# Order of the first token norms, and one token load on ScalarE's queue, in a gated mix of a spectral filter and a token MLP

## The chip, the cores and the metric

The kernel runs on one core of one Trainium2 chip. The metric is the time of one execution on the device in microseconds; the median of several runs is given. The profile is of one further execution, whose span is counted from its first to its last instruction.

## The reference

One tensor of tokens, `x = A_x`, `[1, 2048, 512]` in bfloat16, goes through two branches, a spectral filter over tokens and channels and an MLP over the tokens, and the results are mixed by a gate for each token. Cut to what matters:

```python
x = A_x
g = sigmoid((x * gate_w).sum(-1, keepdims=True))
X = rfft2(x) * (A_w_r + 1j * A_w_i)           # spectral filter
a = irfft2(X, s=(2048, 512))
h = layernorm(x, axis=-1)                   # over the 512 channels, eps 1e-5
u = gelu(einsum("bsd,sf->bdf", h, B_w1) + B_b1) # over the 2048 tokens, f = 1792
b = (einsum("bdf,fs->bds", u, B_w2) + B_b2).transpose(0, 2, 1)
out = g * a + (1 - g) * b
```

The other input `B_x` is not read. The kernel loads the tokens once, through the view `xv`.

## The kernel before

The 2048 tokens are 16 blocks of 128, one token to a partition, 512 channels along the free dimension. Blocks 0 to 7 lie in the buffer `xa` (`xh[0]` in the code), 8 to 15 in `xb`. `load_x(b0, b1)` loads token blocks, `load_w1a(b0, b1)` the rows of `B_w1` for the same blocks and the first 1,024 of its 1,792 columns. All these loads are written out by hand, in the order in which they are to be issued, on SyncE's (SP's) queue. ScalarE's queue carries one small load ahead of them, the first bias `brow`, and near the end one store. Loads share eight completion semaphores in turn, so a load waits, before it is issued, for the landing of the load eight before it.

The order on every engine is the order in which the program calls its instructions (`manual_schedule`). What happens first, and is touched by the change:

- TensorE runs a few matmuls on zeros (`pw`), then `mm1(b, ft)` (line 275) for the blocks 0 to 11 in order: eight matmuls of 128x512 for each block, which need the normalised tokens `hn[:, b]` and the block's weights `w1a`. The last four blocks follow, then the rest of the products and the transforms of the spectral branch, all in one hand-made interleaving (`fill`, `fill_to`, `token`, `dpass`, `inverse`).
- VectorE makes the sums of a block (`bstat`, line 246, `bn_stats` over 512 channels) and aggregates them into mean and variance (`bn_aggr`).
- For the blocks 0 and 1 the root of the variance is taken by ScalarE (line 299, `Sqrt`), and the reciprocal by VectorE (line 304). ScalarE then loads another table (line 306, for `Sin`), and computes angles for the transforms (lines 308 and 309).
- For the later blocks `aggr` (lines 251 to 258) adds epsilon (line 255) and GpSimd takes the power -1/2 (line 258).
- The blocks 0 to 5 are normalised by VectorE (`norm_dve`, line 271; `NDVE` is 6), the blocks 6 to 15 by ScalarE in pairs (`norm`, lines 264 and 267).

The loop over the first two blocks (lines 296 to 305) puts the sums of block 2 between the root of block 1 and its reciprocal: its last lines for block 1 are `bstat(2)`, the reciprocal, and `norm_dve(1)`. After it `aggr(2, 3)` follows, and a loop in which the sums of block b + 1 stand ahead of the norm of block b.

Of the kernel before, what the change touches and what calls it, by code (L numbers as in the profile page):

```python
# [12 lines left out]
F32 = mybir.dt.float32  # L13
I32 = mybir.dt.int32

P = 128
# [6 lines left out]
NDVE = 6  # L23
# [20 lines left out]
def kernel(  # L44
# [13 lines left out]
    nc = tc.nc  # L58
# [5 lines left out]
    small = ctx.enter_context(tc.tile_pool(name="small", bufs=1))  # L64
# [3 lines left out]
    def H(i, shape, name, dt=BF16):  # L68
        return big.tile(shape, dt, tag=f"h{i}", name=name)
# [11 lines left out]
    xv = A_x[0].rearrange("(b a) d -> a b d", a=P)  # L81
    w1v = B_w1.rearrange("(b a) f -> a b f", a=P)
    w2v = B_w2.rearrange("(ft f) s -> f ft s", f=P)
    xh = [H(0, [P, 8, D], "xa"), H(1, [P, 8, D], "xb")]
# [4 lines left out]
    def load_x(b0, b1):  # L89
        nc.sync.dma_start(out=xh[b0 // 8][:, b0 % 8:(b1 - 1) % 8 + 1], in_=xv[:, b0:b1])  # L90

    def load_w1a(b0, b1):
        nc.sync.dma_start(out=w1a[b0 // 4][:, b0 % 4:(b1 - 1) % 4 + 1], in_=w1v[:, b0:b1, 0:FT1 * P])  # L93
# [27 lines left out]
    nc.scalar.dma_start(out=brow[:], in_=B_b1.rearrange("(ft f) -> ft f", f=P))  # L121
    load_w1a(0, 1)
    load_x(1, 2)
    for b in range(1, 3):
        load_x(b + 1, b + 2)
        load_w1a(b, b + 1)
    load_x(4, 6)
    load_w1a(3, 4)
    load_x(6, 8)
# [97 lines left out]
    stats = small.tile([P, NB, nc.vector.BN_STATS_DIM], F32, name="stats")  # L227
    mv = small.tile([P, NB, nc.vector.BN_AGGR_DIM], F32, name="mv")
# [16 lines left out]
    def bstat(b):  # L245
        nc.vector.bn_stats(out=stats[:, b, :], in_=xh[b // 8][:, b % 8, :])  # L246

    def on_dve(b):
        return b <= NDVE or b == NB - 2

    def aggr(b0, b1):
        for b in range(b0, b1):
            nc.vector.bn_aggr(out=mv[:, b, :], in_=stats[:, b, :])
        eng = nc.vector if on_dve(b0) else nc.gpsimd
        eng.tensor_scalar(mv[:, b0:b1, 1], mv[:, b0:b1, 1], 1e-5, 0.0, op0=Alu.add, op1=Alu.add)  # L255
        if not on_dve(b0):
            nc.gpsimd.tensor_scalar(nmr[:, b0:b1], mv[:, b0:b1, 0], -1.0, 0.0, op0=Alu.mult, op1=Alu.add)
        nc.gpsimd.tensor_tensor(rstd[:, b0:b1], mv[:, b0:b1, 1], c_mhalf.to_broadcast([P, b1 - b0]), op=Alu.pow)  # L258
# [11 lines left out]
    def norm_dve(b):  # L270
        nc.vector.tensor_scalar(hn[:, b, :], xh[0][:, b, :], mv[:, b, 0:1], rstd[:, b:b + 1],  # L271
                                op0=Alu.subtract, op1=Alu.mult)
# [14 lines left out]

    sink = small.tile([P, 1], F32, name="sink")
    nc.scalar.activation(sink[:], consts[:, 5:6], ActF.Sqrt, bias=consts[:, 5:6], scale=1.0)
    for v in range(2):  # L290
        nc.vector.tensor_scalar(md[:, v], lrow[:], acol[:, 1:2], 768.0 * v, op0=Alu.mult, op1=Alu.add)


    bcol = small.tile([P, NFT + NB], F32, name="bcol")
    b1f, b2f = bcol[:, 0:NFT], bcol[:, NFT:]
    for b in range(2):
        bstat(b)
        nc.vector.bn_aggr(out=mv[:, b, :], in_=stats[:, b, :])
        nc.scalar.activation(rstd[:, b:b + 1], mv[:, b, 1:2], ActF.Sqrt, bias=consts[:, 5:6], scale=1.0)
        if b == 0:  # L300
            nc.scalar.copy(b1f, pb[:, 0:NFT])
        else:
            bstat(2)
        nc.vector.reciprocal(rstd[:, b:b + 1], rstd[:, b:b + 1])
        norm_dve(b)
    nc.scalar.activation(sink[:], consts[:, 2:3], ActF.Sin, bias=c_mpi, scale=0.0)
# [2 lines left out]
    nc.scalar.activation(mc[:], acol[:, 0:1], ActF.Identity, bias=consts[:, 4:5], scale=1024.0)  # L309


    aggr(2, 3)
    for b in range(2, NDVE):
        bstat(b + 1)
        norm_dve(b)
        if b + 1 < NDVE:
            aggr(b + 1, b + 2)
    for b in range(NDVE, NB, 2):
        if b > NDVE:
            bstat(b)  # L320
        if b == NDVE + 2:
            norm(b - 2, b)
            sines_d()
        bstat(b + 1)
        aggr(b, b + 2)
        if b == NDVE:
            mask(md[:], 1024)
        if b == NB - 2:
            angles_a(1)
        if b > NDVE:  # L330
            norm(b, b + 2)
        if b == NB - 6:
            angles_a(0)
            sines_a(0)
# [4 lines left out]
    for q in range(4):  # L339
# [8 lines left out]
                                in_=TD[:].rearrange("p s t k -> p (s t k)"))  # L348
    nc.sync.dma_start_transpose(out=TB[:].rearrange("p s t k -> p (s t) k"),
                                in_=TA[:].rearrange("p s t k -> p (s t k)"))  # L350
# [445 lines left out]
    b = NB - 1  # L796
# [36 lines left out]
```

## Time and profile before

| | |
|---|---|
| median of 3 runs | 128.57 us (128.41 to 129.02) |
| the profiled execution | 128.94 us |
| its span | 127.2 us, granted clock 1.0 |
| TensorE busy | 122.1 us (96%) |
| VectorE busy | 111.4 us (88%) |
| ScalarE busy | 89.6 us (70%) |
| GpSimd busy | 39.3 us (31%) |
| DMA | 24.05 MB, mean 189 GB/s |

Lines of the profile name an engine, a line of the kernel, the operation, what it writes and reads, and its form; in a timeline the first two numbers are the start and the length in microseconds from the span's start, and a row that ends in "x3" holds three instructions. Square brackets give the idle time ahead of it and what ended that. A matmul's drawn end is modelled and lies beyond the point at which the next one may start: matmuls of 128x512 follow each other every 0.216 us, while each is drawn 0.38 long. PE is TensorE, DVE VectorE, ACT ScalarE, POOL GpSimd, and SPq or ACTq the queue of an engine that issues a DMA. Landings of loads are the times at which the sixteen DMA engines have raised the load's semaphore.

### The profile page before, as it was taken

Reading aid. Unit: us, or ns where it says so; the run is one execution under the profiler, and the core shown is the slowest. Engines: PE = TensorE matmul, PEld = TensorE weight load, DVE = VectorE, ACT = ScalarE, POOL = GpSimd, SP = SyncE. Lnnn points to the kernel's source line nnn. Section 1 sums busy time; section 2 is a strip of 40 time slices with the busy share of each in tenths; the row PEclk is TensorE's granted clock in tenths of the full one; section 3 lists DMA queues with packets and bytes.
Section 4 is the critical chain, followed back from the end, with each engine's and each line's share of the span. In section 5 each row is a group of like instructions: output and inputs, shape, how many; then the busy total and the mean of one; then the engine's idle time right before and its main releaser. Section 6 shows DMA issues by size and latency. Waiting matters only on the chain.

```text
span 127.2 us, 2074 instructions
## 1 busy us (share of the span) xinstructions
PE 122.1 (96%) x750; PEld 65.1 (51%) x750; DVE 111.4 (88%) x190; ACT 89.6 (70%) x137; POOL 39.3 (31%) x67
## 2 busy tenths in 40 slices
PE   6989999999999999999999999999999999999980
PEld 2234444444444576557764765477644444444570
DVE  3699998999999999999999999999999999992150
ACT  4391299999897689998994799229794599422410
POOL 7124288998839397000030000000000000351200
PEclk9999999999999999999999999999999999999999
DMA  3899999998799999999579306710021101179991
GB/s 103 257 312 384 370 372 350 288 302 273 205 226 177 312 289 293 290 288 290 140 208 295 74 0 179 238 42 0 0 83 45 41 18 48 61 93 209 163 219 24
DMA packets 34635, 24.05 MB, mean 189 GB/s; under 512 B 5536, under 2 KB 32032, under 8 KB 34624
## 3 DMA queue, kind: packets, MB, share of 16 engines
q1 hardware_dynamic: 32516, 21.02, 60.0%
q0 software_dynamic: 1936, 2.76, 13.0%
q10 hardware_dynamic: 172, 0.13, 0.3%
q8 instruction: 6, 0.10, 0.3%
q14 instruction: 5, 0.04, 0.1%
HBM read 19.15 MB, written 3.67 MB: 179 GB/s over the span
## 4 chain that ended last, share of the span: by engine, by line
PE 91%; DMA 3%; DVE 1%; SPq 1%; issue 0%
PE yb L469 36%; PE u L275 20%; PE u L459 16%; PE ivt L658 5%; DMA xa<-in_A_x_dram 3%; PE ivd L674 3%; PE dp L526 3%; PE yb L801 2%; PE tok L517 2%; PE tok L518 2%; SPq L90 1%; DVE stats L246 1%; PE ivt L652 0%; PE tok L514 0%; SPq L93 0%; DVE hn L271 0%
## 5 line engine op out<-in xcount | busy, mean ns | idle before, releaser
L469 PE MATMUL yb<-gl,w2t 128*128 128x512 bf16 x210 | 47.5, 379 | 0.0
L469 PEld LDWEIGHTS <-w2t 128*128 128x128 bf16 x210 | 20.2, 98 | 22.0
L275 PE MATMUL u<-hn,w1a 128*128 128x512 bf16 x128 | 28.3, 382 | 0.5 <-DVE hn L271 0.4
L459 PE MATMUL u<-hn,w1b 128*128 128x512 bf16 x96 | 23.3, 379 | 0.0
L449 ACT ACTIVATE tbv<-yb,ombb,omg 128x512 bf16<-128x512 f32 x15 | 11.6, 775 | 15.6 <-PE yb L469 15.6
L275 PEld LDWEIGHTS <-w1a 128*128 128x128 bf16 x128 | 12.6, 98 | 16.3 <-issue 1.5
L779 POOL DMA_DIRECT2D out_dram<-ap x3 | 4.0, 1528 | 49.3 <-DVE ap L774 45.3
L459 PEld LDWEIGHTS <-w1b 128*128 128x128 bf16 x96 | 9.0, 98 | 8.0
L286 ACT ACTIVATE junk<-prod 128x512 bf16<-128x512 bf16 x16 | 10.1, 631 | 0.3
L355 ACT ACTIVATE gl<-u,bcol 128x512 bf16<-128x512 f32 x14 | 9.2, 687 | 1.3 <-PE u L459 0.8
L630 ACT CAST R<-ivt 128x1024 bf16<-128x1024 f32 x8 | 7.8, 1040 | 2.3 <-PE ivt L658 2.3
L258 POOL TENSOR_TENSOR rstd<-mv,consts 128x2 f32<-128x2 f32 (+1 forms) x9 | 6.3, 703 | 8.2 <-DVE mv L255 8.1
L630 ACT CAST H<-ivd 128x1024 bf16<-128x1024 f32 x7 | 6.9, 1050 | 0.8 <-PE ivd L674 0.8
L246 DVE BATCH_NORM_STATS2 stats<-xa 128x6 f32<-128x512 bf16 x8 | 5.5, 686 | 1.1 <-DMA xa<-in_A_x_dram 1.1
L788 DVE TENSOR_TENSOR tbv<-tbv,ap 128x512 bf16<-128x512 bf16 x3 | 1.3, 425 | 5.7 <-ACT tbv L449 5.7
L267 ACT ACTIVATE hn<-xb,nmr,rstd 128x512 bf16<-128x512 bf16 x8 | 5.8, 800 | 0.0
L548 DVE TENSOR_TENSOR tatb<-PMA,wn 128x1024 bf16<-128x1024 bf16 x8 | 5.0, 690 | 0.2 <-issue 0.2
L267 ACT ACTIVATE hn<-xa,nmr,rstd 128x512 bf16<-128x512 bf16 x2 | 1.5, 806 | 5.2 <-DVE nmr L264 5.2
L246 DVE BATCH_NORM_STATS2 stats<-xb 128x6 f32<-128x512 bf16 x8 | 5.2, 675 | 0.0
L674 PEld LDWEIGHTS <-R 128*128 128x128 bf16 x64 | 3.8, 98 | 2.5 <-ACT R L630 2.5
L548 DVE TENSOR_TENSOR tatb<-PMB,wn 128x2048 bf16<-128x2048 bf16 x4 | 4.7, 1227 | 0.2
L674 PE MATMUL ivd<-TI,R 128*128 128x128 bf16 x64 | 4.9, 220 | 0.0
(198 smaller groups left out, 224.5 us busy)
## 6 DMA issues: line engine op xcount, KB each, us to landing
w2t<-in_B_w_dram SPq DMA_DIRECT2D x8, 896.0 KB, 9.8
w1b<-in_B_w_dram SPq DMA_DIRECT2D x3, 1024.0 KB, 16.2
w1a<-in_B_w_dram SPq DMA_DIRECT2D x2, 1024.0 KB
out_dram<-tbv SPq DMA_DIRECT2D x14, 128.0 KB, 3.9
out_dram<-ap POOLq DMA_DIRECT2D x3, 512.0 KB, 6.5
w1a<-in_B_w_dram SPq DMA_DIRECT2D x4, 256.0 KB, 4.6
w1a<-in_B_w_dram SPq DMA_DIRECT2D x2, 512.0 KB, 7.9
xb<-in_A_x_dram SPq DMA_DIRECT2D x2, 512.0 KB, 7.2
```

The costliest lines, as they stand in the source:

```text
L246: nc.vector.bn_stats(out=stats[:, b, :], in_=xh[b // 8][:, b % 8, :])
L267: nc.scalar.activation(hn[:, b, :], xh[b // 8][:, b % 8, :], ActF.Identity, bias=nmr[:, b:b + 1], scale=rstd[:, b:b + 1])
L275: nc.tensor.matmul(u1[ft], lhsT=w1a[b // 4][:, b % 4, ft * P:(ft + 1) * P], rhs=hn[:, b, :], start=(b == 0), stop=(b == NB - 1))
L286: nc.scalar.activation(junk[:], prod[b // 8][:, b % 8], ActF.Copy, accum_out=glog[:, b:b + 1])
L355: nc.scalar.activation(gl[:, ft, :], src, ActF.Gelu_apprx_tanh, bias=b1f[:, ft:ft + 1], scale=1.0)
L449: nc.scalar.activation(tbv[0][:, b], y[:], ActF.Identity, bias=gate["ombb2"][:, b:b + 1], scale=gate["omg"][:, b:b + 1])
L459: nc.tensor.matmul(u[:], lhsT=w1b[c][:, b, k * P:(k + 1) * P], rhs=hn[:, b, :], start=(b == 0), stop=(b == NB - 1))
L469: nc.tensor.matmul(y[:], lhsT=w2t[b // 2][:, ft, (b % 2) * P:(b % 2 + 1) * P], rhs=gl[:, ft, :], start=(ft == 0), stop=(ft == NFT - 1))
L548: mul(tt[:, i, :, r:r + n], PM[:, 2 * s:2 * s + 2, r:r + n], w[:, None].to_broadcast([P, 2, n, 256]))
L630: nc.scalar.copy(out, pr[:].rearrange("p h n -> p (h n)"))
L658: nc.tensor.matmul(o[:, 2 * v:2 * v + 2], lhsT=UV[:, 2 * v + c, r, par::2], rhs=TB[:, s, c:c + 2], start=(c == 0), stop=(c == 1))
L674: nc.tensor.matmul(pr[:, c, o * P:(o + 1) * P], lhsT=plane(par, cos), rhs=TI[:, lst, t], start=True, stop=True)
```

## The change

Tokens of block 2 are issued by ScalarE, after its first activation, and leave SP's queue; the weights of block 1 take their place there, one issue earlier. The loop over the first blocks runs over three: block 1 is normalised before the sums of block 2 start, and block 2 takes its root on ScalarE and its reciprocal on VectorE as the first two do. The sums of block 3 are made in two halves of 256 channels in a buffer of their own, `st3`; the first half stands between block 2's aggregation and its reciprocal, the second behind block 2's norm. One `bn_aggr` takes both halves. From block 3 on GpSimd's power is used as before.

```diff
     load_w1a(0, 1)
     load_x(1, 2)
-    for b in range(1, 3):
-        load_x(b + 1, b + 2)
-        load_w1a(b, b + 1)
+    load_w1a(1, 2)
+    load_x(3, 4)
+    load_w1a(2, 3)
     load_x(4, 6)
...
         for b in range(b0, b1):
-            nc.vector.bn_aggr(out=mv[:, b, :], in_=stats[:, b, :])
+            nc.vector.bn_aggr(out=mv[:, b, :], in_=stats[:, b, :] if b != 3 else st3[:])
...
     nc.scalar.activation(sink[:], consts[:, 5:6], ActF.Sqrt, bias=consts[:, 5:6], scale=1.0)
+    nc.scalar.dma_start(out=xh[0][:, 2], in_=xv[:, 2])
...
-    for b in range(2):
+    st3 = small.tile([P, 2, nc.vector.BN_STATS_DIM], F32, name="st3")
+
+    def bstat3(h):
+        nc.vector.bn_stats(out=st3[:, h, :], in_=xh[0][:, 3, 256 * h:256 * h + 256])
+
+    for b in range(3):
         bstat(b)
         nc.vector.bn_aggr(out=mv[:, b, :], in_=stats[:, b, :])
         nc.scalar.activation(rstd[:, b:b + 1], mv[:, b, 1:2], ActF.Sqrt, bias=consts[:, 5:6], scale=1.0)
         if b == 0:
             nc.scalar.copy(b1f, pb[:, 0:NFT])
-        else:
-            bstat(2)
+        if b == 2:
+            bstat3(0)
         nc.vector.reciprocal(rstd[:, b:b + 1], rstd[:, b:b + 1])
         norm_dve(b)
     nc.scalar.activation(sink[:], consts[:, 2:3], ActF.Sin, bias=c_mpi, scale=0.0)
...
-    aggr(2, 3)
-    for b in range(2, NDVE):
+    bstat3(1)
+    aggr(3, 4)
+    for b in range(3, NDVE):
         bstat(b + 1)
         norm_dve(b)
```

## The prediction

> **What bounds the kernel now.** The profiled execution took 128.94 us; its span is 127.2, and 1.74 lie around it. The median of three runs is 128.57. I sum against 128.94 and carry the difference over to the median.
>
> I read the chain that ended last first (start, length, what):
>
> ```profile
> 2.13 4.10 DMA xa<-in_A_x_dram
> 6.25 0.69 DVE stats L246
> 7.05 0.42 DVE hn L271
> 7.51 26.06 PE u L275 x120
> ```
>
> From 7.51 on the chain is TensorE alone: 120 matmuls in 26.06 us are 0.217 each, and among the matmul records up to the last product no two starts lie more than 0.31 apart. So whatever moves TensorE's work at 7.51 moves the end, and nothing else touched by the change does. Ahead of 7.51 the chain is the load of token block 2, its sums, and then the norm of block 1. VectorE's timeline shows why block 2 stands there:
>
> ```profile
> 4.71 0.68 DVE L246 BATCH_NORM_STATS2 stats<-xa 128x6 f32<-128x512 bf16 x1
> 5.42 0.18 DVE L298 BATCH_NORM_AGGREGATE mv<-stats 128x2 f32<-128x6 f32 x1
> 6.25 0.69 DVE L246 BATCH_NORM_STATS2 stats<-xa 128x6 f32<-128x512 bf16 x1 [0.65 <-DMA xa<-in_A_x_dram]
> 6.87 0.15 DVE L304 RECIPROCAL rstd<-rstd 128x1 f32<-128x1 f32 x1
> 7.05 0.41 DVE L271 TENSOR_SCALAR hn<-xa,mv,rstd 128x512 bf16<-128x512 bf16 x1
> ```
>
> Block 1 is aggregated at 5.60 and ScalarE's root for it ends at 5.93, but the reciprocal sits behind the sums of block 2, which wait for a load that lands at 6.22. TensorE pays for it:
>
> ```profile
> 6.26 0.81 PE L275 MATMUL u<-hn,w1a 128*128 128x512 bf16 x3
> 7.51 0.38 PE L275 MATMUL u<-hn,w1a 128*128 128x512 bf16 x1 [0.44 <-DVE hn L271]
> ```
>
> The last matmul of block 0 starts at 6.69 (three of them, 0.216 apart, from 6.26). Its successor could start at 6.91 and starts at 7.51: the hole is **0.60 us**, not the 0.44 shown, since a matmul's drawn end is later than its slot's. It is the most that the change can bring.
>
> Next, what is late after it. TensorE takes a block (eight matmuls) every 1.727 us, and I compared the end of each block's norm with the start of its first matmul: spare time 0.39 us at block 2, 0.75, 1.12, 1.49 at blocks 3 to 5, then **0.14 at block 6**, and 0.66 or more from block 7 on. Block 6 is the first that ScalarE normalises:
>
> ```profile
> 15.00 0.16 DVE L264 SCALAR_TENSOR_TENSOR nmr<-mv,rstd 128x2 f32<-128x2 f32 x1
> 15.19 1.52 ACT L267 ACTIVATE hn<-xa,nmr,rstd 128x512 bf16<-128x512 bf16 x2 [5.20 <-DVE nmr L264]
> 15.93 0.60 PE L275 MATMUL u<-hn,w1a 128*128 128x512 bf16 x2
> ```
>
> The first of ScalarE's two ends at 16.00 and TensorE's block 6 starts at 16.14 (the second matmul of the last line). A start follows its norm by 0.05 at least (7.46 to 7.51), so 0.09 is left. Before it stands VectorE's chain, without a pause from 7.05 to 15.00. TensorE therefore keeps of the 0.60 only 0.09 plus what VectorE's chain itself gains.
>
> **The change part by part.**
>
> *Block 1's norm before block 2's sums.* The root ends at 5.93; the reciprocal follows by 0.03, the norm by 0.19, and the next instruction by 0.33 (4.38 to 4.71). So the norm runs 6.16 to 6.57 instead of 7.05 to 7.46, and block 2's sums may start at 6.48. TensorE can take block 1 at 6.91 if its weights are there: they landed at 6.88 (the weight load at 6.93 waited for them), issued at 2.60 as the fifth load. Now they are the fourth, at 2.13, and no tokens of block 2 are ahead of them: about 6.4.
>
> *Block 2's root on ScalarE.* It adds a round trip and removes one on GpSimd. Sums 6.48, aggregate 0.72 later at 7.20, root 0.22 later, 7.42 to 7.72, reciprocal 7.75, norm 7.94 to 8.35 (before 8.44 to 8.85). The pause of VectorE from 7.32 to 7.75 is filled by the first half of block 3's sums. No row has a half sum. A whole one is 0.68 long and lets the next start 0.58 later (15.89 to 16.47); instructions on a single column take 0.15 (L255), so 512 elements take the other 0.53 and 256 some 0.27: by this estimate a half is 0.42 long and holds the engine 0.31. The bounds are 0.29, half a whole one, and 0.58, as much as a whole one. At 0.31 the first half is wholly covered. The second starts at 8.27; aggregate 8.72, the addition of L255 8.93, block 4's sums 9.00. They started at 9.05 (9.04 by the records): **VectorE gains 0.04 us**, because two half sums, the reciprocal and the longer wait cost nearly what the wait for the load cost. If a half costs as much as a whole, they start at 9.41, 0.37 later.
>
> ScalarE's table load (1.28) and the two angle activations (2.36) slide behind that root, from 5.95 to 7.72, and end near 11.8 instead of 9.99. ScalarE is idle for 5.20 us before block 6's norm at 15.19, and the mask that reads them is at 17.28: 3.4 us of cover, cost nothing. Without it the norm of block 6 would be later by 1.8.
>
> *Block 2's tokens on ScalarE's queue.* ScalarE issues them after its first activation, near 2.72. Its two issues in the trace took 0.65 and 0.39, so it is free by 3.37; its root of block 0 is at 3.85, and 0.48 is left before it would hold up everything. Landing: a load on an empty queue takes 2.15 (block 0: 0.72 to 2.87), and ScalarE's last store put its first packet out 1.03 after the issue. From 3.75, eight packets of 46 ns on each DMA engine, taking turns with eight of SP's of 84, are 1.04, and 0.3 to the semaphore: about 5.1. But on five of the sixteen engines block 2's load came in 0.5 to 1.4 behind the rest (4.81 to 6.22), and that would make 6.5. I take **5.9**, since the DMA engines have room then:
>
> ```profile
> 3.50:4.50 1.00, 1.00 (x4) 0.23 (x3) 0.57 (x4) 0.47 (x2) 0.15 (x1) 1.00 0.68 215
> 4.50:5.50 1.00, 0.96 (x3) 0.25 (x2) 0.97 (x3) 0.00 (x0) 0.00 (x0) 1.00 0.71 207
> ```
>
> (the last two columns are the DMA share and GB/s; later it is 1.07 and 377). It is needed at 6.48: nothing is paid. Each microsecond beyond would be paid in full.
>
> The Trainium skill, DMA: Bandwidth & Descriptors, speaks to this twice. In "Queues, rings and completion order" each DMA engine goes round-robin between the queues that have work, which is the turn-taking above. In "Issuing engines are not separate DMA queues" issuing from several engines saves only the sequencer's issue time; by that alone the tokens would come no sooner than behind all that SP has issued, which is the first rival.
>
> *SP's queue.* Without that load each later issue is 0.47 earlier up to the sixth. From the eighth on each waits for the load eight before: tokens 8 to 11 now for block 1's weights, and the weights of blocks 6 and 7 for ScalarE's load. Those were issued at 6.24 and 6.90 and landed at 13.47 and 14.82, some 7 us of queue: a delay of a few tenths is absorbed. Block 3's tokens landed at 7.23 and are needed by 7.43; fewer bytes are now ahead.
>
> *Sum.* TensorE starts block 1 at 6.91, runs 0.60 ahead to the end of block 5, and waits 0.47 at block 6, whose norm ends at 15.96: start 16.01 against 16.14. Gain 0.09 + 0.04 = 0.13 us. Span 127.07, the execution 128.81, on the median **128.44 us**.
>
> **The rivals.**
>
> *Tokens late (slower).* If ScalarE's load lands behind SP's, it comes with the last of the same 1,024 KB, which landed at 7.23. Block 2's sums then start at 7.26, 0.78 late, block 6's norm ends at 16.74, TensorE's block 6 starts at 16.79: 0.65 later, **129.22**. It decides from a landing of 6.6 on. For it: SP's loads of that time took 4.1 to 4.3 us, five engines lagged; 2.72 + 4.2 is 6.9. Against: DMA engines idle for a third of that time, and the bias load that ScalarE issued together with block 0 landed at 2.46, before it.
>
> *The whole hole closes.* Should block 6's chain be shorter (its power on GpSimd took 0.94 where the next took 0.70, beside VectorE's mask), TensorE keeps more, up to 0.60: **127.97**. Against: VectorE's own sums up to 14.99 gate the next step anyway.
>
> *Halves cost like wholes.* Then block 6 starts 0.28 after its old time: **128.85**; at no gain at all 128.57. For it: only that no row shows a half.
>
> **How the numbers follow.** The forecast 0.60, tokens late 0.20, the whole hole 0.10, costly halves 0.10. A median of this kernel can tell some 0.5% (0.64 us) from no change. The hole is smaller than that, so faster by over 0.5% needs the run-to-run scatter besides (128.41 to 129.02): 0.06. Slower by over 0.5% is the late half of the first rival and what I have not seen: 0.16. Within: 0.78. The range goes from the whole hole, 128.0, to the late tokens at 7.23, 129.2.
>
> **What would show it.** Right: block 1's matmuls from 6.91, a wait of about 0.47 for ScalarE's norm at block 6, block 4's sums near 9.00, block 2's sums at 6.48 with no wait for DMA. Wrong: block 2's sums waiting for their tokens, block 6 starting after 16.14, a half sum over 0.5 us, ScalarE's root of block 0 later than 3.85 behind its issue.

## The result, and the profile after

The changed kernel takes **129.37 us** in the median (129.04 to 130.73, 14 runs), the kernel before, on the same chip, 128.78 (128.41 to 129.44, 14 runs). The ratio is 1.0052 with a 95% interval of 1.0029 to 1.0074: slower by 0.6 us. The forecast was 128.44, the range 128.0 to 129.2; the result lies outside. The profiled execution of the changed kernel took 129.12 us, its span is 127.3.

The chain that ended last, of the changed kernel (start, length, what). Before, it went from block 2's load over its sums and block 1's norm to TensorE at 7.51, and stayed there:

```profile
1.66 3.16 DMA xa<-in_A_x_dram
4.84 0.70 DVE stats L246
...
15.39 0.82 ACT hn L267
16.26 17.43 PE u L275 x80
```

It now begins with another load, the tokens of **block 1**, and reaches TensorE only at block 6. TensorE's timeline of the changed kernel says the same. By the starts of the matmuls the hole ahead of block 1 has shrunk from 0.60 to 0.19, too little to show in rows whose drawn ends are late, and a wait stands ahead of block 6:

```profile
4.87 10.93 PE L275 MATMUL u<-hn,w1a 128*128 128x512 bf16 x48 [0.27 <-DVE hn L271]
16.26 2.54 PE L275 MATMUL u<-hn,w1a 128*128 128x512 bf16 x11 [0.46 <-ACT hn L267]
```

Block 1's matmuls start at 6.78 instead of 7.51, block 6's at 16.26 instead of 16.14. What lies between is VectorE's timeline:

```profile
4.84 0.69 DVE L246 BATCH_NORM_STATS2 stats<-xa 128x6 f32<-128x512 bf16 x1
5.57 0.18 DVE L304 BATCH_NORM_AGGREGATE mv<-stats 128x2 f32<-128x6 f32 x1
6.12 0.16 DVE L310 RECIPROCAL rstd<-rstd 128x1 f32<-128x1 f32 x1 [0.36 <-ACT rstd L305]
6.32 0.41 DVE L271 TENSOR_SCALAR hn<-xa,mv,rstd 128x512 bf16<-128x512 bf16 x1
6.64 0.69 DVE L246 BATCH_NORM_STATS2 stats<-xa 128x6 f32<-128x512 bf16 x1
7.37 0.18 DVE L304 BATCH_NORM_AGGREGATE mv<-stats 128x2 f32<-128x6 f32 x1
7.47 0.39 DVE L300 BATCH_NORM_STATS2 st<-xa 128x6 f32<-128x256 bf16 x1
7.91 0.17 DVE L310 RECIPROCAL rstd<-rstd 128x1 f32<-128x1 f32 x1
8.11 0.41 DVE L271 TENSOR_SCALAR hn<-xa,mv,rstd 128x512 bf16<-128x512 bf16 x1
8.44 0.42 DVE L300 BATCH_NORM_STATS2 st<-xa 128x6 f32<-128x256 bf16 x1
8.89 0.21 DVE L253 BATCH_NORM_AGGREGATE mv<-st 128x2 f32<-128x12 f32 x1
9.14 0.15 DVE L255 TENSOR_SCALAR mv<-mv 128x1 f32<-128x1 f32 x1
9.21 0.68 DVE L246 BATCH_NORM_STATS2 stats<-xa 128x6 f32<-128x512 bf16 x1
```

Block 1's sums start at 4.84, 0.13 later than before (4.71). From there to block 4's sums (the last row) it is 4.37 by these rows, and nothing in it waits for a load. Block 2's tokens were there long before: ScalarE's timeline shows when they were issued.

```profile
1.41 1.28 ACT L289 ACT_TABLE_LOAD   x1 [1.41 <-PEq L824]
1.48 0.36 ACTq L290 DMA_DIRECT2D xa<-in_A_x_dram  x1
2.71 0.29 ACT L289 ACTIVATE sink<-consts 128x1 f32<-128x1 f32 x1
```

The activation of line 289 stands ahead of the load in the program. It runs at 2.71; the load went out at 1.48, while the engine was still loading a table, and **ahead of block 1's load**, which SP issues at 1.66. Block 2's tokens landed at 4.65, block 1's at 4.82; before it was 6.22 and 4.36.

### The profile page after: what moved, and what is told of

It reads as the page before. It is cut to its first block, busy times and chain, and to the rows that moved or that the text cites. A ratio compares the mean times of both kernels' runs of the same rounds, so it can differ in the third digit from the quotient of the medians.

```text
span 127.3 us, 2074 instructions
## 1 busy us (share of the span) xinstructions
PE 122.0 (96%) x750; PEld 65.0 (51%) x750; DVE 111.8 (88%) x191; ACT 89.9 (71%) x138; POOL 37.8 (30%) x66
## 4 chain that ended last, share of the span: by engine, by line
PE 84%; DVE 6%; DMA 2%; POOL 1%; ACT 1%; issue 1%; SPq 1%
PE yb L476 36%; PE u L466 16%; PE u L275 14%; PE ivt L665 5%; PE ivd L681 3%; PE dp L533 3%; DMA xa<-in_A_x_dram 2%; PE yb L808 2%; PE tok L524 2%; PE tok L525 2%; DVE stats L246 2%; DVE hn L271 2%; POOL rstd L258 1%; ACT hn L267 1%; DVE mv L255 1%
## 5 line engine op out<-in xcount | busy, mean ns | idle before, releaser
L258 POOL TENSOR_TENSOR rstd<-mv,consts 128x2 f32<-128x2 f32 (+1 forms) x8 | 5.8, 722 | 9.0 <-DVE mv L255 8.9
L246 DVE BATCH_NORM_STATS2 stats<-xa 128x6 f32<-128x512 bf16 x7 | 4.8, 687 | 0.5 <-DMA xa<-in_A_x_dram 0.5
L526 ACT CAST ZA<-tok 128x1024 bf16<-128x1024 f32 x4 | 4.0, 1018 | 1.4 <-PE tok L525 1.3
## 6 DMA issues: line engine op xcount, KB each, us to landing
out_dram<-tbv SPq DMA_DIRECT2D x14, 128.0 KB, 4.0
```

## The experiments

Four theories stood against each other. **A**: the early load on ScalarE's queue makes block 1's tokens late, and a chain without slack hands that on. **B**: the new order on VectorE is dear in itself. **C**: the loss lies elsewhere, behind block 6. **D**, from the second batch on: the one trace of before had caught a late load, so that the hole was no fixed loss, and the order is judged against a better kernel than that trace shows.

"New loads" are block 2's tokens on ScalarE's queue with SP's list as changed; "new order" is VectorE's and ScalarE's part of the change. Medians are of 11 or 12 runs where several were made; each ratio is against the kernel before on the same chip (its medians 128.69 to 128.86). Landings and starts are from the one trace of each, landings cut to hundredths.

**The change as it stands, twice.** No edit.

> The changed kernel once more, for a second trace. Theory A (the early load): ScalarE issues block 2's tokens at 1.47 us, beside the loads of blocks 0 and 1 on the same DMA engines; block 1's tokens land late (4.82 against 4.36 in the first traces), VectorE's whole chain shifts, and with it block 6's norm: its matmuls start 0.1 to 0.5 us later than the 16.14 of the kernel before. Theory B (the reorder is dear in itself: ScalarE's root for block 2 and two half sums cost VectorE more than they spare): block 6 is late by about 0.1, however the tokens land. Theory C (the loss lies elsewhere): block 6 at 16.25, and the distance from there to the end of the span is longer than the 111.0 of the kernel before. Time 129.2 to 129.6 by all three.

> The changed kernel, for a third trace. Theory D: block 1's tokens land at 4.7 to 5.1, behind the 4.1 to 4.4 of the old loads; block 1's sums start with that landing and block 4's 4.36 later; block 6's norm ends 7.0 after those and its matmuls start 0.05 behind. If block 1's tokens land by 4.7, the execution takes 129.0 and the rest of the loss is elsewhere.

Measured: 129.28 (128.81 to 129.69), 1.0037 (1.0015 to 1.0060); the later single execution 129.49. Block 1's sums on VectorE, the first and then the later:

```profile
5.09 0.69 DVE L246 BATCH_NORM_STATS2 stats<-xa 128x6 f32<-128x512 bf16 x1 [0.24 <-DMA xa<-in_A_x_dram]
```
```profile
5.17 0.69 DVE L246 BATCH_NORM_STATS2 stats<-xa 128x6 f32<-128x512 bf16 x1 [0.34 <-DMA xa<-in_A_x_dram]
```

Here the wait for the load is written out: block 1's tokens landed at 5.07 and 5.14. Block 4's sums followed 4.36 after those of block 1 in all three traces of the changed kernel, block 6's norm ended 7.00 after that. The profiled times, less the start of block 1's sums (4.84, 5.09, 5.17), are 124.28, 124.27 and 124.32: over three executions that start alone sets the time.

**The loads alone.** The order is that of before.

```diff
-    for b in range(1, 3):
-        load_x(b + 1, b + 2)
-        load_w1a(b, b + 1)
+    load_w1a(1, 2)
+    load_x(3, 4)
+    load_w1a(2, 3)
...
+    nc.scalar.dma_start(out=xh[0][:, 2], in_=xv[:, 2])
```

> The new loads with the old order of sums and norms. A: block 1's tokens land at 4.8 and its sums start 0.14 late, but block 2's tokens are there as well, so its sums follow at 5.7 instead of 6.25 without a wait; block 1's norm ends at 6.9, block 4's sums start near 8.5 instead of 9.04, block 6's norm ends near 15.45, its matmuls start at 15.55: 0.55 to 0.6 faster than the kernel before. B: as fast, since the loads are harmless. C: as slow as the changed kernel, if the loads or the queue cost something behind the start.

Measured: 128.47 (127.79 to 129.62), 0.9990 (0.9966 to 1.0014). The sums of blocks 1, 2, and 4 on VectorE:

```profile
4.83 0.69 DVE L246 BATCH_NORM_STATS2 stats<-xa 128x6 f32<-128x512 bf16 x1
5.66 0.66 DVE L246 BATCH_NORM_STATS2 stats<-xa 128x6 f32<-128x512 bf16 x1
...
8.42 0.68 DVE L246 BATCH_NORM_STATS2 stats<-xa 128x6 f32<-128x512 bf16 x1
```

Block 1 is as late as in the changed kernel (landing 4.80), yet block 4's sums come 3.59 after it instead of 4.36, and TensorE waits at neither block 1 nor block 6. The changed kernel, in the same batch, is 0.81 behind this one: the order costs that on the new loads.

**The order alone.** The loads are those of before.

```diff
-    load_w1a(1, 2)
-    load_x(3, 4)
-    load_w1a(2, 3)
+    for b in range(1, 3):
+        load_x(b + 1, b + 2)
+        load_w1a(b, b + 1)
...
-    nc.scalar.dma_start(out=xh[0][:, 2], in_=xv[:, 2])
```

> The old loads (block 2's tokens on SP's queue as its fourth) with the new order. A: block 1's tokens land at 4.36 again, its norm runs from 6.16, block 2's sums from 6.48, block 4's from 9.04, block 6's matmuls start at 16.1: within 0.1 of the kernel before, and 0.15 to 0.5 faster than the changed kernel. B: as slow as the changed kernel. C: the same as the kernel before if the loads are the cause, as the changed one if not.

Measured: 128.88, 1.0017 (1.0000 to 1.0035). Sums of blocks 1, 2 and 4:

```profile
4.59 0.69 DVE L246 BATCH_NORM_STATS2 stats<-xa 128x6 f32<-128x512 bf16 x1
6.38 0.69 DVE L246 BATCH_NORM_STATS2 stats<-xa 128x6 f32<-128x512 bf16 x1
...
8.94 0.68 DVE L246 BATCH_NORM_STATS2 stats<-xa 128x6 f32<-128x512 bf16 x1
```

Block 1's tokens landed at 4.27, and the chain was 4.35 again. By the medians the order alone is 0.19 slower than before (the interval reaches 1), and the whole change 0.40 slower than the order alone: with this order the new loads lose 0.40, and with the old order they lose nothing on balance (128.47 against 128.69). A and B both have a share. Block 2's tokens, on SP's queue as before, landed here at 5.47, not at 6.22; that raised D.

**Whole sums for block 3, in the changed kernel.**

```diff
-            nc.vector.bn_aggr(out=mv[:, b, :], in_=stats[:, b, :] if b != 3 else st3[:])
+            nc.vector.bn_aggr(out=mv[:, b, :], in_=stats[:, b, :])
...
         if b == 2:
-            bstat3(0)
+            bstat(3)
...
-    bstat3(1)
     aggr(3, 4)
```

> The changed kernel, but block 3's sums in one piece of 512 channels between block 2's aggregation and its reciprocal. The whole sum delays the reciprocal by 0.13 (next start 0.58 after 7.46 instead of the root's end at 7.87), and spares the second half with its wait, 8.44 to 8.89: block 4's sums start 0.3 to 0.35 earlier than in the changed kernel, near 8.87, block 6's matmuls near 15.9. A: 0.25 to 0.35 faster than the changed kernel, on the same tokens' landings. B: the same, and more if the halves are the whole of the loss. C: no change at the end.

Measured: 128.99, 1.0023 (1.0001 to 1.0045). Sums of blocks 1, 3 and 4:

```profile
4.75 0.69 DVE L246 BATCH_NORM_STATS2 stats<-xa 128x6 f32<-128x512 bf16 x1
...
7.38 0.66 DVE L246 BATCH_NORM_STATS2 stats<-xa 128x6 f32<-128x512 bf16 x1
8.75 0.68 DVE L246 BATCH_NORM_STATS2 stats<-xa 128x6 f32<-128x512 bf16 x1
```

From block 1 to block 4 it is 3.99 instead of 4.36: the two halves cost 0.37 more than one whole, because the second half has nothing to hide behind (8.44 to 8.89 in the changed kernel's rows). The median is 0.29 lower than that of the changed kernel.

**The kernel before, two more traces.** No edit; what is asked is when block 2's tokens land.

> The kernel before, for a second trace. Theory D (the first trace caught a late load): block 2's tokens land nearer to 5.5 than to 6.22 as a rule; the sums of block 2 start then, block 1's norm ends 1.21 after that start, and block 1's matmuls start at the later of 6.91 and that end plus 0.05. With a landing of 5.5 the hole of 0.60 is gone and the execution takes about 128.4; with 5.9 it takes 128.65. The rival (the hole belongs to the kernel): landing near 6.2, the hole near 0.6, 128.9.

> The same again. Theory D: another landing, and the time moves with it as in the run ahead of this: 128.35 plus whatever the landing exceeds 5.6 by. The rival: 6.2 and 128.9.

Measured: 129.53 and 128.66, one execution each. Sums of block 2 and block 4, first in the second trace of before, then in the third:

```profile
5.73 0.69 DVE L246 BATCH_NORM_STATS2 stats<-xa 128x6 f32<-128x512 bf16 x1
...
9.81 0.69 DVE L246 BATCH_NORM_STATS2 stats<-xa 128x6 f32<-128x512 bf16 x1 [1.20 <-DMA xa<-in_A_x_dram]
```
```profile
6.12 0.69 DVE L246 BATCH_NORM_STATS2 stats<-xa 128x6 f32<-128x512 bf16 x1 [0.48 <-DMA xa<-in_A_x_dram]
...
8.91 0.69 DVE L246 BATCH_NORM_STATS2 stats<-xa 128x6 f32<-128x512 bf16 x1
```

In the second the wait for block 2's tokens is not there at all (landing 5.70), and TensorE runs from block 1 through block 2 without a hole; a late load of blocks 4 and 5 (9.78) holds VectorE up for 1.20 instead, TensorE then waits at blocks 3, 4 and 6, and the execution misses the 128.4 to 128.65 that had been expected. In the third the hole ahead of block 1 is 0.41. The hole of 0.60 was no fixed loss: it was one draw, and the largest of the three (0.60, none, 0.41).

**Two other ways to place the loads, in the old order.** Both start from the loads alone. In the first, block 1's tokens ride on ScalarE's queue and block 2's take their place on SP's; in the second, block 1's tokens go ahead of block 0's weights.

```diff
-    load_x(1, 2)
+    load_x(2, 3)
...
-    nc.scalar.dma_start(out=xh[0][:, 2], in_=xv[:, 2])
+    nc.scalar.dma_start(out=xh[0][:, 1], in_=xv[:, 1])
```

> The old order of sums and norms; block 1's tokens on ScalarE's queue at 1.47 instead of block 2's, which take their place on SP's as the third load at 1.66. Theory A+D: whichever of the two is on ScalarE's queue lands at 4.5 to 4.9, the other at 4.7 to 5.1; block 1's sums start at 4.7 to 4.85 and block 2's at 5.6, with no wait worth naming; no hole ahead of block 1, block 6 without a wait: 128.2 to 128.4, like the kernel with the loads only, and 0.2 to 0.4 under the kernel before. If sharing costs the one on SP's queue alone, block 1's sums start at 4.70 here and nothing else changes.

```diff
-    load_w1a(0, 1)
     load_x(1, 2)
+    load_w1a(0, 1)
```

> The old order of sums and norms; on SP's queue block 1's tokens ahead of block 0's weights (0.72, 1.19, then the weights at 1.66 and 2.13), block 2's on ScalarE's queue. Theory A+D: block 1's tokens land before 4.0 and block 2's by 4.6, so no sums wait for a load; block 0's weights land at 4.3 to 4.8 and are needed at 4.85. If they are in time: 128.2 to 128.4, with less scatter than the loads alone, as no late landing is left on the chain. If they are late by x, TensorE starts later by x, of which the wait ahead of block 1 (none or some tenths) is all that can hide it.

Measured: 128.38 (127.89 to 129.19), 0.9971 (0.9947 to 0.9995); and 128.51 (128.08 to 130.72), 0.9975 (0.9957 to 0.9994). Both are faster than the kernel before, by 0.3%, with intervals that just clear 1; the changed kernel was slower than it in both of its batches. In the first, block 1's sums, and TensorE from block 1 on:

```profile
5.18 0.69 DVE L246 BATCH_NORM_STATS2 stats<-xa 128x6 f32<-128x512 bf16 x1 [0.43 <-DMA xa<-in_A_x_dram]
...
7.24 10.95 PE L275 MATMUL u<-hn,w1a 128*128 128x512 bf16 x50 [0.54 <-DVE hn L271]
```

Block 1 lands at 5.15, as late as in the worst trace of the changed kernel, but block 4's sums follow after 3.59 at 8.77, and block 6 does not wait. The late load is not free in the old order either: TensorE waits for block 1's norm, with a hole of 0.71 by the matmuls' starts, and the kernel's last matmul starts 0.30 later than with the loads alone (123.09 against 122.79), whose block 1 landed at 4.80. But block 6 starts some 10.7 after block 1's sums here (15.87 - 5.18), in the changed kernel 11.4 (16.26 - 4.84): both orders hand a load this late on, and the new one has the longer way behind it. In the second, block 1's tokens land at 3.47 and block 4's sums start at 8.30, the earliest of all; TensorE's first row shows the price, block 0's weights landing at 4.95:

```profile
5.00 13.77 PE L275 MATMUL u<-hn,w1a 128*128 128x512 bf16 x63 [0.44 <-DMA w1a<-in_B_w_dram]
```

**The changed kernel with block 1's tokens ahead of block 0's weights.** It is the edit just above in the changed kernel.

> The changed kernel, but block 1's tokens as the second load on SP's queue, ahead of block 0's weights, so that the early load on ScalarE's queue no longer holds them up. Theory D (VectorE's chain from block 1's sums to block 4's is 4.36 long in the new order, and 3.59 in the old one if no load is late): block 1's sums start at 4.6 to 4.7 as soon as block 0's norm is issued, block 4's 4.36 later at 9.0, block 6's matmuls near 16.05: 128.8 to 128.9, 0.4 faster than the changed kernel and within 0.2 of the kernel before; the order still costs its 0.77 against the old order with the same loads (128.51). Rival (it was only the late tokens): with the tokens early the new order is as fast as the old one, 128.3 to 128.5.

Measured: 129.10 (128.58 to 132.9), 1.0013 (0.9979 to 1.0048). Block 1's tokens landed at 4.24, its sums started at 4.66 and block 4's at 9.01, 4.35 later; block 6's matmuls start at 16.07 instead of 16.26. So the trace bears the expected chain out, but the median misses the 128.8 to 128.9 and leaves the question open: the runs scatter by 4 us, and block 0's weights, now behind, landed at 5.41 in the trace. The wide scatter was not explained.

**The move alone.** In the kernel before, the sums of block 2 go behind block 1's norm; GpSimd's power and whole sums stay.

```diff
-        else:
-            bstat(2)
...
+    bstat(2)
     aggr(2, 3)
```

> The kernel before with one line moved: block 2's sums behind block 1's norm. Old loads, block 2's power on GpSimd, whole sums. Theory D: from block 1's sums 1.79 to block 2's sums and from there the old 2.79: block 4's sums start 4.58 after block 1's, near 9.28, unless block 2's tokens land after 6.48; block 6's matmuls near 16.35. That is 0.22 more than with ScalarE's root and two halves: 129.0 to 129.2, 0.2 to 0.4 slower than the kernel before. Rival (moving the norm ahead is right, and ScalarE's root and the halves are what costs): faster than the order of the change, 128.6 or less.

Measured: 128.87, 1.0016 (0.9987 to 1.0044). Block 1's sums start at 4.68, block 4's at 8.88: 4.20, where 4.58 had been expected. The expectation had counted the reciprocal and norm of block 1 twice (they lie inside the old stretch from block 2's sums to block 4's, 2.79, of which 2.41 remain). So the move itself costs 4.20 - 3.59 = 0.61, ScalarE's root instead of GpSimd's power gives back 0.21 (3.99), and the halves take 0.37 (4.36).

**The new order with whole sums and the old loads.** It is the kernel with whole sums above, with the load list of before and without the load on ScalarE's queue.

> Old loads, the new order with ScalarE's root for block 2, but block 3's sums in one piece. Theory D: block 4's sums start 3.99 after block 1's (4.36 with halves, 4.20 with the reorder alone): at 8.65 to 8.7, if block 2's tokens land by 6.45; block 6's matmuls near 15.7. The kernel before reaches that only where block 2's tokens land by 5.9. So 128.5 to 128.7, 0.2 to 0.4 faster than the same with halves (128.88) and about even with the kernel before or 0.2 under it. Rival (a half sum costs half of a whole, so that two halves and one whole are even but for 0.06): 128.85.

Measured: 128.99 (128.5 to 130.32), 1.0018 (0.9988 to 1.0047); 128.5 to 128.7 had been expected. The trace has block 4's sums waiting:

```profile
9.49 0.69 DVE L246 BATCH_NORM_STATS2 stats<-xa 128x6 f32<-128x512 bf16 x1 [0.68 <-DMA xa<-in_A_x_dram]
```

The tokens of blocks 4 and 5 landed at 9.46; by the chain the sums would have started near 8.74 (4.75 + 3.99). A shorter chain gains nothing in an execution in which its next load is late. Whether that was so in most of the timed runs, the one trace can't say; by the medians whole sums gained nothing over halves on the old loads (128.99 against 128.88).

**Block 2's tokens issued later.** What stayed open was whether block 1's tokens come back when block 2's load starts behind theirs, and what that is worth. GpSimd issues it at 2.15, in the new order and in the old one.

```diff
+    nc.gpsimd.dma_start(out=xh[0][:, 2], in_=xv[:, 2])
     iota(krow[:, 0], [[8, 2], [16, 64]], 0)
...
-    nc.scalar.dma_start(out=xh[0][:, 2], in_=xv[:, 2])
```

> The changed kernel, but block 2's tokens are issued by GpSimd behind its comparison for ident, near 2.2 us, instead of by ScalarE at 1.47: later than block 1's load on SP (1.66), and off SP's queue as well. Theory (the early issue holds block 1's tokens up): block 1's tokens land at 4.1 to 4.4 again, block 1's sums start at 4.70 behind block 0's norm, block 4's 4.36 later at 9.06, or at the landing of block 4's tokens (8.0 to 8.8) if that is later; block 6's matmuls near 16.1: 128.8 to 128.95, 0.35 to 0.5 faster than the changed kernel. Rival (any load beside SP's queue, or the new order on SP's queue, holds block 1's tokens up): they land at 4.8 to 5.1 and the time is 129.3.

> The same loads with the old order of sums and norms. Theory: block 1's tokens at 4.1 to 4.4; block 2's, issued near 2.2, land by 5.5, so their sums start at 5.6 without a wait; block 4's sums 3.59 after block 1's, at 8.3, or at the landing of block 4's tokens; block 6 without a wait: 128.2 to 128.5, 0.5 under the same loads in the new order. Rival: if GpSimd's load lands after 6.2, it is no better than the kernel before, 128.8.

Measured: 129.35 (128.86 to 130.42), 1.0045 (1.0023 to 1.0067), and 129.90 (128.97 to 130.5), 1.0071 (1.0047 to 1.0094). Sums of blocks 1 and 2 in the new order:

```profile
4.69 0.69 DVE L247 BATCH_NORM_STATS2 stats<-xa 128x6 f32<-128x512 bf16 x1
7.73 0.69 DVE L247 BATCH_NORM_STATS2 stats<-xa 128x6 f32<-128x512 bf16 x1 [1.17 <-DMA xa<-in_A_x_dram]
```

Block 1's tokens landed at 4.17 and 4.49 in the two traces, near those of the old loads (4.14 to 4.38 in six) and ahead of those of the new ones (4.72 to 5.14 in five). That is A's mechanism shown by its removal, in one trace of each order. Block 2's, however, land at 7.70 and 6.42 through GpSimd's queue, and the wait is paid in full: block 4's sums follow those of block 2 by 2.57, as in the changed kernel, and block 6 starts at 17.36 in the new order. Both medians miss what had been expected (128.8 to 128.95, and 128.2 to 128.5), and fit the late landing in sign; that the old order's is the worse of the two, and 0.65 above its own profiled execution (129.25), is not explained.

## Why the prediction was wrong, and where it was right

**What holds now.** In the new order with its halves block 4's sums start 4.36 after block 1's (4.35 to 4.37), or 2.57 after block 2's where those wait for their tokens; in the old one they start at the later of block 1's sums + 3.59 and block 2's sums + 2.79, and in either not before the tokens of blocks 4 and 5. Block 6's norm ends 6.95 to 7.01 later (6.79 to 6.87 in the three traces where block 4's sums had to wait for their tokens), and where its matmuls wait for it they start 0.05 behind. In every trace where block 6 waits, the last matmul of the kernel starts 107.27 after that norm: all behind it is shifted whole, so C falls.

**The first step that failed: the state of before.** The working took block 2's landing at 6.22, and with it the hole, as what the kernel pays each time. On the old loads and SP's queue it landed at 5.47, 5.70, 5.77, 6.09, 6.13 and 6.22 in six traces: the trace of before is the latest. The new order pays 0.77 of chain (4.36 - 3.59) in every execution to be rid of a wait that only some have. With block 1's sums at 4.70 it breaks even when block 2's sums start at 4.70 + 4.36 - 2.79 = 6.27, which is a landing near 6.24, just about the one that was used. That is why the sum came out near nothing; the 0.13 gained against this one trace was then taken off the median, as if every execution had its hole. At the median landing, 5.93, the old order has block 4's sums at 8.75 and the new one at 9.06: 0.3 worse. TensorE itself, in the trace of before, was ready for block 6 only 0.09 after its norm allowed it, so some 0.2 of that is lost at the end. The order alone measured 0.19 slower, which its interval does not tell apart from nothing.

**The second: the issue on ScalarE's queue.** "ScalarE issues them after its first activation, near 2.72" took the order in the program for the order in time. The load went out at 1.48 and took a share of the 16 DMA engines from block 1's: in the trace of the changed kernel its 128 packets of 1 KB run from 3.08 to 4.26, among 186 of SP's queue. The prediction went through the cost of the load for every step but block 1's own. Those tokens landed at 4.82, 5.07 and 5.14 in the changed kernel, and block 1's sums started 0.14, 0.39 and 0.47 behind 4.70, each handed on to the end in full; their mean is 0.33. The old order would have handed part of that on too, at block 1, but there the early tokens of block 2 paid for it. The two together, 0.2 + 0.33, stand against the 0.6 that the medians show, and against 0.19 + 0.40 from the order alone and the loads on top of it. In the profiled pair alone the loss is small (129.12 against 128.94), since there the best of three landings of after stands against the worst of three waits of before for block 2.

The Trainium skill, DMA: Bandwidth & Descriptors, says in "Queues, rings and completion order" that a DMA engine goes round-robin between the queues that have work. The trace agrees: block 1's tokens land at 4.72 to 5.14 where block 2's are issued ahead of them on ScalarE's queue, and at 4.14 to 4.38 where all are on SP's. The same page, in "Issuing engines are not separate DMA queues", holds that issuing from several engines saves only sequencer time. The rival that was built on it, tokens no sooner than SP's, is the opposite of what came: 4.65 to 4.98 in the changed kernel instead of 5.47 to 6.22. Nor was the sequencer's time all that changed. From 3.5 to 5.5 the DMA engines moved 166 to 233 GB/s in the six traces with all these loads on SP's queue, and 274 to 340 in the eight with one load of tokens on ScalarE's. Here the measurement decides: the second queue came with more bytes moved. SP's later loads go out one issue (0.47) earlier there, but they do so too with GpSimd's load, where it was 189 and 243; why the second queue moves more was not found.

**The rivals.** *Tokens late* had the right kind of mechanism and the wrong block: block 2's came early, block 1's late. *The whole hole closes* needed a shorter chain to block 6; it did not come. *Halves cost like wholes*: a half is 0.39 to 0.42 long where 0.42 was estimated, so each is no whole, but the pair costs 0.37 more than one whole; the working never priced the pair against that alternative.

**What was right.** VectorE's chain from block 1 to block 4 was put at 4.30 and measured 4.36. The wait goes from block 1 to block 6 (matmuls of block 1 from 6.78, predicted 6.91; a gap of 0.62 at block 6, predicted 0.47). ScalarE's angles ended near 11.9 and cost nothing. The chain was worked out right; its start, and what it was compared with, were not.

## What to carry to other kernels

A wait for a load seen in one trace is one draw. Before work is added to every execution to dodge it, take the landing from several traces, and compute at which landing the new order breaks even. And the load on ScalarE's queue did not wait here for the activation written ahead of it: look for the load next in line, which it overtakes, and for who waits for that one. The new loads with the order left alone came out even with the kernel before (128.47 against 128.69, the interval across 1); the two other placements in the old order, both with block 2's tokens sooner (5.34 and 4.77), measured 128.38 and 128.51 against 128.86.

## What the runs showed of the hardware that was not expected

- ScalarE's queue put out a load at 1.48, during a table load from 1.41 to 2.69, ahead of the activation at 2.71 that stands before it in the program.
- The landings of the first loads scatter between executions of the same list: block 2's 128 KB from 5.47 to 6.22 in six traces, the tokens of blocks 4 and 5 from 8.51 to 9.78 in the same traces. Why single DMA engines come in late was not found.
- A load of 128 KB issued by GpSimd at 2.15 landed at 7.70 and 6.42, where ScalarE's, issued at 1.48, landed between 4.49 and 5.21 in eight traces.
- With one such load on ScalarE's queue beside SP's, the DMA engines moved 274 to 340 GB/s from 3.5 to 5.5 (eight traces), without it 166 to 233 (six).
